# First expert's weights: w1 halves one per group in groups 1 to 8, w2 halves in pairs from group 15 to the tail

## The chip, the cores and the metric

The kernel runs on one core of a Trainium2 chip. The metric is the device time of one execution in microseconds, the median of the runs. Five engines work from queues of their own: TensorE (PE, with PEld for its weight loads), VectorE (DVE), ScalarE (ACT), GpSimd (POOL) and SyncE (SP, which here only issues DMAs). All DMAs share 16 DMA engines.

## The reference, cut to what matters

Attention in chunks of 64 rows gives 4608 rows of 512 numbers. Each row is then sent to the one of 8 experts whose gate logit is largest:

```
x = attn_out.transpose(0, 2, 1, 3).reshape(4608, 512)
logits = x @ w_gate
expert_idx = argmax(logits, axis=1)
for e in range(8):
    xe = x[expert_idx == e]
    h = maximum(xe @ w1[e], 0)        # w1[e]: 512 x 1024
    out[expert_idx == e] = gate_w * (h @ w2[e])   # w2[e]: 1024 x 512
```

## The kernel before, in words

**Attention, groups 0 to 17.** The 36 tiles of 128 rows are worked in 18 groups of two tiles (the loop over `g` at L1003). Group g computes the scores of its own tiles, transposes the probabilities of group g-1 (`attn_t`), multiplies them by V (`attn_v`), writes the result into a ring of row buffers `xb` (`x_out`), and transposes and projects the rows of group g-2 on the gate (`x_t`, `logits`). After the loop comes a tail, written out by hand from L1042, in which the last groups' steps alternate with pieces of the first expert's two matrix products (`filler`, 32 half steps in all, from `slot_0`).

**Routing and stores.** When a batch of 6 or 4 tiles has its logits, `route` computes each row's place in the sorted order, in small VectorE steps that `small_op` deals out. From then on `store` (L434) writes the rows to DRAM, one GpSimd indirect DMA for each tile (L441), at most two for each call; `store(2, after)` first has ScalarE copy one element of `after` into the row (L439), so that GpSimd doesn't send the row before that point. The row numbers of a batch lie in `di` (L418), a tile with two buffers, so a batch's `di` is written over the one of two batches before. After the last store, `gather(1)` (L1113, L569) reads the rows of slot 1 back in sorted order; `make_xt(1)` transposes them on PE (L591) and slot 1 begins. Slots 1 and up are the rest of the span.

**Weights of the first expert.** w1[0] and w2[0] lie in DRAM as four blocks of 128 x 2048; each is loaded in four pieces of 128 x 512 (256 KB), by `load_q(j)` on SP, where j = 0 to 7 is w1 and j = 8 to 15 is w2. They land in two staging buffers `raw[0]` and `raw[1]`; piece j uses the place of piece j-8 again. `split_half` makes two float32r tiles of a piece: ScalarE casts it (L84, the high part) and GpSimd subtracts that from the piece (L85, the low part). `cast(g)` (L996) first splits the pieces listed for g and then loads those listed for g. In the loop it is called behind the softmax of the group (L1027). w1 is needed from the first filler on, w2 from the fourth step of `slot_0`.

**Order.** PE, DVE, ACT and POOL keep the order in which the program lists their instructions. SP's queue holds, for each group, `cast`'s loads, then `load_qk(g+3)` (gated by the scores of group g, which free the buffer), then `load_v(g+2)` (gated by `attn_v` of group g-1). `cast`'s loads wait only for the staging place.

Of the kernel before, what the change touches and what calls it, by code (L numbers as in the profile page):

```python
# [47 lines left out]
def attn_moe_kernel(ctx: ExitStack, tc: tile.TileContext, q, k, v, wg, w, out):  # L48
# [31 lines left out]
    def split_half(c, m, buf, eng=None):  # L80

        hi, lo = w_hi[0][c][:, m * 512:(m + 1) * 512], w_lo[0][c][:, m * 512:(m + 1) * 512]
        src = raw[buf][:, (c % 2) * 1024 + m * 512:(c % 2) * 1024 + (m + 1) * 512]
        nc.scalar.copy(hi, src)  # L84
        (eng or nc.gpsimd).tensor_tensor(lo, src, hi.bitcast(F32), ALU.subtract)  # L85
# [13 lines left out]
    def bank(tag, shape):  # L99
        n = 1  # L100
        for x in shape[1:]:
            n *= x
        if tag == "S":
            t = psum[0].tile([P, 512], F32, name="psS", tag="S", bufs=2)
        else:
            t = slots[tag][turns[tag] % len(slots[tag])]
            turns[tag] += 1
        t = t[0:shape[0], 0:n]
        if len(shape) == 3:
            t = t.rearrange("p (a b) -> p a b", b=shape[2])  # L110
        return t
# [194 lines left out]
    def x_out(g, px, ri, xt):  # L306
        r0 = g * G % RB

        t = g * G - XB * RB
        assert t < 0 or t in stored  # L310
        for m in range(2):
            nc.vector.tensor_tensor(
                xt[:, r0:r0 + G, m * 256:(m + 1) * 256].rearrange("p i (h d) -> p i h d", d=64),
                px[m].rearrange("p (i h d) -> p i h d", i=G, d=64),
                ri.rearrange("p (i h m) o -> p i h m o", i=G, m=2)[:, :, :, m, :]
                .broadcast_to([P, G, 4, 64]), ALU.mult)

    def x_t(g, xt):
        xT = sp.tile([P, 4, G * P], F32, name="xT1", bufs=1)
        for i in range(G):  # L320
            pxt = bank("TQ", [P, 4, 128])
            for kc in range(4):
                nc.tensor.transpose(pxt[:, kc, :], xt[:, (g * G + i) % RB, kc * 128:(kc + 1) * 128],
                                    ident)
            nc.scalar.copy(xT[:, :, i * P:(i + 1) * P], pxt)
        return xT
# [4 lines left out]
    def logits_p(g, xT):  # L331

        pp = pL[:, 128:128 + G * P]
        for kc in range(4):
            nc.tensor.matmul(pp[kc * 32:(kc + 1) * 32, :], wg_sb[:, kc, :], xT[:, kc, :],
                             start=True, stop=True, tile_position=(0, kc * 32))
        lp = sp.tile([P, G * P], F32, name="lp", bufs=2)
        return lp, pp
# [95 lines left out]
    def store(n, after=None):  # L434

        for k, (b, i, t, di) in enumerate(waiting[:n]):
            x = xb[t // RB % XB][:, t % RB, :]
            if k == 0 and after is not None:
                nc.scalar.copy(x[:, XW - 1:XW], after)  # L439
            stored.add(t)  # L440
            nc.gpsimd.indirect_dma_start(  # L441
                out=xds[b % 2 * NMAX + i],
                out_offset=bass.IndirectOffsetOnAxis(ap=di[:, i, :], axis=0),
                in_=x, in_offset=None, bounds_check=NT - 1, oob_is_err=False)
        del waiting[:n]
# [4 lines left out]
    def advance(kind, side=False):  # L450


        for x in active:
            if x[1] == kind and x[2] == side and not (kind == "t" and r_live[0]):
                x[1] = next(x[0], "end")
                if x[1] == "end":
                    active.remove(x)
                return
# [3 lines left out]
    def small_op(n=1):  # L462

        for _ in range(min(n, pace[0])):
            advance("v")
            pace[0] -= 1
# [233 lines left out]
    def filler(n):  # L700
        for _ in range(n):
            next(fill, None)
            halves[0] -= 1
# [271 lines left out]
    def logits(g):  # L975
        if g in st_x:
            lp, pp = logits_p(g, st_x.pop(g))
            nc.scalar.copy(lp, pp)
            st_l[g] = lp

    def pauses():
        for x in list(active):
            if x[1] is None:
                x[1] = next(x[0], "end")
                if x[1] == "end":
                    active.remove(x)

    def load_q(j):

        c, s = j // 4, slice(j % 4 * 512, (j % 4 + 1) * 512)  # L990
        nc.sync.dma_start(raw[c % 2][:, s], w[c * E * P:c * E * P + P, s])

    loads = {g: [2 * g - 2, 2 * g - 1] for g in range(1, 9)}
    splits = {g: [2 * g - 6, 2 * g - 5] for g in range(3, 11)}

    def cast(g):  # L996

        for j in splits.get(g, ()):
            split_half(j // 2, j % 2, j // 4 % 2)
        for j in loads.get(g, ()):  # L1000
            load_q(j)
# [46 lines left out]
    g = NG - 1  # L1048
# [10 lines left out]
    soft_e(su)  # L1059
    advance("a")  # L1060
    st_x[g - 1] = x_t(g - 1, xb[(g - 1) * G // RB % XB])
    pauses()
    small_op(7)
    advance("a")
# [4 lines left out]
    ri = soft_d(su)  # L1069
    x_out(g, px, ri, xb[g * G // RB % XB])  # L1070
    logits(g - 1)
    store(2, st_l[g - 1][:, 0:1])
    filler(1)
    advance("t")
# [215 lines left out]
```

## Time and profile before

| what | us |
|---|---|
| median of 3 runs | 584.07 |
| the three runs | 581.40, 584.07, 587.08 |
| the profiled execution, its own time | 583.63 |
| its span | 581.5 |
| PE busy | 561.4 (97%) |
| DVE busy | 443.5 (76%) |
| ACT busy | 300.1 (52%) |
| POOL busy | 275.7 (47%) |

The span is the time from the program's first to its last instruction; 2.1 us of the execution's own time lie around it. Busy times are those of the profiled execution. PE's busy time is made from modelled ends of matmuls, so what counts is where it waits.

### The profile page before, as it was taken

To read this page: it belongs to the slowest core of one execution; us is meant where nothing else is said; L and a number is where in the kernel's file an instruction comes from. 1 tells how busy PE (TensorE), PEld (TensorE's weight loads), DVE (VectorE), ACT (ScalarE), POOL (GpSimd) and SP (SyncE) were. 2 spreads that over 40 slices of the span, in tenths; PEclk is the share of its full clock that TensorE was granted. 3 is DMA by queue.
4 is the path that set the end of the run, shared out by engine and by line. 5 is a ranking of instruction groups with operands and counts; after the bars stand their busy time and mean duration, and the time that the engine had idled before them with its cause. 6 is when DMAs were issued, how large, how long until landed. Compare 5 with 4: busy or idle time off the path is not lost.

```text
span 581.5 us, 13591 instructions
## 1 busy us (share of the span) xinstructions
PE 561.4 (97%) x5047; PEld 498.3 (86%) x5047; DVE 443.5 (76%) x834; ACT 300.1 (52%) x563; POOL 275.7 (47%) x279
## 2 busy tenths in 40 slices
PE   6999998999899999999999999999999999999995
PEld 6788877888788998989889899999988999899894
DVE  8899998976676877786776677877666787778775
ACT  1678755652144554563554455464434555456553
POOL 5056742447543754435355366444614444644352
PEclk9999999999999999999999999999999999999998
DMA  8999999425674732456246423368712245632121
GB/s 280 401 402 387 399 319 308 155 104 197 212 284 138 242 105 64 147 154 210 61 154 204 133 85 86 128 204 298 223 55 93 74 137 153 214 99 75 22 57 38
DMA packets 52510, 103.22 MB, mean 178 GB/s; under 512 B 15712, under 2 KB 32096, under 8 KB 48800
## 3 DMA queue, kind: packets, MB, share of 16 engines
q0 software_dynamic: 20704, 60.74, 30.8%
q1 hardware_dynamic: 31680, 40.93, 21.0%
q8 instruction: 63, 1.03, 0.7%
q14 instruction: 63, 0.52, 0.3%
HBM read 121.60 MB, written 19.82 MB: 243 GB/s over the span
## 4 chain that ended last, share of the span: by engine, by line
PE 67%; DMA 17%; issue 7%; POOL 4%; POOLq 3%; DVE 1%; ACT 0%; SPq 0%; DVEq 0%; ACTq 0%
PE psS L635 12%; DMA out_y<-y,oid 10%; PE psS L642 6%; PE psS L245 6%; DMA raw<-in_w,widx 6%; PE psV L713 4%; PE psU L713 4%; PE psU L714 3%; PE psL L635 3%; PE psV L714 3%; PE psU L715 3%; PE psV L715 3%; PE psU L300 3%; POOLq L1228 3%; POOL raw L551 2%
## 5 line engine op out<-in xcount | busy, mean ns | idle before, releaser
L78 DVE TENSOR_TENSOR wlo<-raw,whi 128x1024 fp32r<-128x1024 f32 x134 | 163.4, 1219 | 27.5 <-ACT whi L77 24.5
L77 ACT CAST whi<-raw 128x1024 fp32r<-128x1024 f32 x134 | 140.0, 1045 | 0.1
L551 POOL DMA_INDIRECT raw<-in_w,widx x70 | 89.0, 1271 | 103.1 <-DVE wlo L78 49.7
L635 PE MATMUL psS<-xhl,whi 128*128 128x256 f32 x688 | 127.3, 283 | 0.5 <-DVE xhl L594 0.3
L656 ACT ACTIVATE hh<-psS 128x256 fp32r<-128x256 f32 x110 | 42.3, 385 | 163.7 <-PE psS L635 115.7
L635 PEld LDWEIGHTS psS<-xhl,whi 128*128 128x128 f32 x688 | 111.7, 191 | 7.1 <-DVE xhl L594 0.5
L741 POOL DMA_INDIRECT out_y<-y,oid x40 | 49.5, 1237 | 103.4 <-ACT y L738 24.6
L635 PE MATMUL psS<-xhl,wlo 128*128 128x256 f32 x344 | 97.3, 283 | 0.0
L661 DVE SCALAR_TENSOR_TENSOR hl<-psS,hh 128x256 fp32r<-128x256 f32 x110 | 46.4, 422 | 49.0 <-ACT hh L656 31.0
L569 POOL DMA_INDIRECT xg<-xd,idx x58 | 69.6, 1199 | 22.6 <-issue 14.4
L635 PEld LDWEIGHTS psS<-xhl,wlo 128*128 128x128 f32 x344 | 65.6, 191 | 0.0
L713 PE MATMUL psU<-whi,hh 128*128 128x512 f32 x144 | 57.2, 397 | 1.2 <-ACT xhl L618 1.2
L713 PE MATMUL psV<-whi,hh 128*128 128x512 f32 x144 | 57.5, 399 | 0.3
L714 PE MATMUL psU<-wlo,hh 128*128 128x512 f32 x144 | 56.9, 395 | 0.0
L714 PE MATMUL psV<-wlo,hh 128*128 128x512 f32 x144 | 56.4, 392 | 0.0
L715 PE MATMUL psV<-whi,hl 128*128 128x512 f32 x144 | 56.2, 390 | 0.0
L715 PE MATMUL psU<-whi,hl 128*128 128x512 f32 x144 | 56.2, 390 | 0.0
L441 POOL DMA_INDIRECT xd<-xb,di x32 | 31.5, 985 | 22.8 <-issue 13.3
L635 PE MATMUL psL<-xhl,whi 128*128 128x256 f32 x208 | 38.5, 283 | 0.0
L642 PE MATMUL psS<-xhl,whi 128*128 128x320 f32 (+1 forms) x192 | 36.7, 316 | 0.5 <-ACT xhl L626 0.5
L85 POOL TENSOR_TENSOR wlo<-raw,whi 128x512 fp32r<-128x512 f32 x16 | 20.1, 1276 | 35.1 <-DMA spare<-in_k 20.4
L635 PEld LDWEIGHTS psL<-xhl,whi 128*128 128x128 f32 x208 | 33.2, 191 | 1.1
(244 smaller groups left out, 1082.6 us busy)
## 6 DMA issues: line engine op xcount, KB each, us to landing
qt<-in_q SPq DMA_DIRECT2D x17, 512.0 KB
xg<-xg SPq DMA_DIRECT2D x256, 32.0 KB
vb<-in_v SPq DMA_DIRECT2D x12, 512.0 KB
kb<-in_k SPq DMA_DIRECT2D x22, 256.0 KB
raw<-in_w SPq DMA_DIRECT2D x16, 256.0 KB
spare<-in_k SPq DMA_DIRECT2D x12, 256.0 KB
spare<-in_v SPq DMA_DIRECT2D x6, 512.0 KB
raw<-in_w,widx POOLq DMA_INDIRECT x70, 3.0
```

Of the source, the lines that this page charges most:

```text
L77: nc.scalar.copy(hi, src)
L78: nc.vector.tensor_tensor(lo, src, hi.bitcast(F32), ALU.subtract)
L551: nc.gpsimd.indirect_dma_start(out=raw[c][:, :], out_offset=None, in_=w, in_offset=bass.IndirectOffsetOnAxis(ap=widx[:, u, c:c + 1], axis= ...
L569: nc.gpsimd.indirect_dma_start(out=t[:, :], out_offset=None, in_=xd[0:rows, :], in_offset=bass.IndirectOffsetOnAxis(ap=place(u, h), axis=0 ...
L635: nc.tensor.matmul(ph, a, b[:, kc, 0:BLK], start=kc + i == 0, stop=kc + i == 5)
L642: nc.tensor.matmul(ph, a[par][kc][:, f * 128:(f + 1) * 128], b[:, kc, 0:BLK + n], start=kc + i == 0, stop=kc + i == 5)
L656: nc.scalar.activation(hh, ph, AF.Relu)
L661: nc.vector.scalar_tensor_tensor(hl, ph, 0.0, hh.bitcast(F32), ALU.max, ALU.subtract)
L713: nc.tensor.matmul(py, hh, wh, start=f == 0, stop=False)
L714: nc.tensor.matmul(py, hh, wl, start=False, stop=False)
L715: nc.tensor.matmul(py, hl, wh, start=False, stop=f == 7)
L741: nc.gpsimd.indirect_dma_start(out=outs[m], out_offset=bass.IndirectOffsetOnAxis(ap=oid[u % 3][0:n, m:m + 1], axis=0), in_=y, in_offset=No ...
```

## The change

Loads: in groups 1 to 8 one piece in place of two, so that these groups load w1 alone. The eight pieces of w2 are listed in pairs for g = 15, 16, 17 and 18. Splits: in groups 3 to 10 one piece in place of two; the pairs of w2 for g = 16, 17, 18 and 19. As the loop ends with g = 17, the tail gets two new calls of `cast`: `cast(18)` (there g is 17, so `cast(g + 1)`) behind the transpose `x_t` of group 16, and `cast(19)` behind the logits of group 16, ahead of the `store` that stands there. `cast(18)` splits two pieces and loads the last two; `cast(19)` splits the last two.

```diff
-    loads = {g: [2 * g - 2, 2 * g - 1] for g in range(1, 9)}
-    splits = {g: [2 * g - 6, 2 * g - 5] for g in range(3, 11)}
+    loads = {**{g: [g - 1] for g in range(1, 9)}, **{g: [2 * g - 22, 2 * g - 21] for g in range(15, 19)}}
+    splits = {**{g: [g - 3] for g in range(3, 11)}, **{g: [2 * g - 24, 2 * g - 23] for g in range(16, 20)}}
...
     st_x[g - 1] = x_t(g - 1, xb[(g - 1) * G // RB % XB])
+    cast(g + 1)
     pauses()
     small_op(7)
     advance("a")
...
     logits(g - 1)
+    cast(g + 2)
     store(2, st_l[g - 1][:, 0:1])
```

## Rows read from the trace of the kernel before

**Rows 1.** Busy time by stage: attention, tail, slots (us, engines busy, clock, DMA share, GB/s).

```profile
5.60:112.40 106.80, 100.21 (x2048) 84.44 (x2050) 96.31 (x176) 67.81 (x152) 45.42 (x59) 1.00 0.95 349
112.40:152.50 40.10, 37.62 (x413) 32.44 (x411) 28.09 (x108) 15.30 (x50) 23.29 (x31) 1.00 0.37 139
152.50:581.50 429.00, 420.12 (x2554) 378.19 (x2554) 314.74 (x551) 215.66 (x361) 201.96 (x163) 0.99 0.44 139
```

**Rows 2.** The same view, one row per group: groups 6, 7 and 10 to 14.

```profile
40.63:46.97 6.34, 6.34 (x135) 5.50 (x137) 6.20 (x11) 4.33 (x11) 2.51 (x2) 1.00 1.04 398
46.97:52.99 6.02, 6.02 (x127) 5.02 (x128) 5.75 (x10) 5.03 (x13) 4.47 (x7) 1.00 0.98 375
...
65.38:71.97 6.59, 6.29 (x127) 5.17 (x128) 5.68 (x10) 5.34 (x14) 4.86 (x7) 1.00 1.02 399
71.97:78.27 6.30, 6.13 (x126) 5.04 (x128) 5.97 (x12) 4.83 (x11) 4.69 (x5) 1.00 0.95 339
78.27:85.28 7.01, 6.40 (x136) 5.46 (x137) 6.37 (x14) 4.01 (x10) 2.40 (x5) 1.00 0.92 299
85.28:92.37 7.09, 6.09 (x127) 5.10 (x128) 5.36 (x11) 3.82 (x10) 1.95 (x2) 1.00 0.94 295
92.37:100.04 7.67, 6.18 (x126) 5.12 (x128) 6.63 (x16) 3.83 (x10) 2.14 (x3) 1.00 0.97 339
```

**Rows 3.** The chain that ended last, in group 14 (start, us, what).

```profile
94.63 1.49 issue
```

**Rows 4.** Timeline of SP: last w issue and the last two V.

```profile
52.95 1.35 SPq L991 DMA_DIRECT2D raw<-in_w  x2
...
99.56 0.33 SPq L221 DMA_DIRECT2D spare<-in_v  x1
105.90 0.33 SPq L221 DMA_DIRECT2D vb<-in_v  x1
```

**Rows 5.** Timeline of POOL in the tail (start, us, what, idle before and its end).

```profile
122.82 0.31 POOL L420 COPY xb<-ft 128x4 f32<-128x4 f32 x2 [3.80 <-DVE dst L413]
125.92 0.98 POOL L441 DMA_INDIRECT xd<-xb,di  x1 [2.79 <-ACT xb L439]
127.20 0.98 POOL L441 DMA_INDIRECT xd<-xb,di  x1 [0.31 <-DVE hl L661]
128.97 0.97 POOL L441 DMA_INDIRECT xd<-xb,di  x1 [0.79 <-issue]
...
132.04 0.98 POOL L441 DMA_INDIRECT xd<-xb,di  x1 [0.51 <-POOL xb L420]
...
143.84 0.98 POOL L441 DMA_INDIRECT xd<-xb,di  x1 [0.31 <-issue]
147.56 1.04 POOL L569 DMA_INDIRECT xg<-xd,idx  x1 [2.74 <-PE psS L635]
```

**Rows 6.** PE's timeline at the end of the tail.

```profile
149.84 0.39 PE L715 MATMUL psV<-whi,hl 128*128 128x512 f32 x1
151.05 0.75 PE L591 MATMUL psQ<-ident,xg 128*128 128x128 f32 x4 [0.82 <-DMA xg<-xd,idx]
```

**Rows 7.** The two instructions of a split, all 16 (ns min/median/max, first and last start).

```profile
L84 ACT CAST whi<-raw x16: 602/617/631, 28.6 to 72.4; 128x512 fp32r<-128x512 f32 x16
L85 POOL TENSOR_TENSOR wlo<-raw,whi x16: 1265/1276/1286, 29.3 to 73.8; 128x512 fp32r<-128x512 f32 x16
```

**Rows 8.** ACT's timeline in group 17 and where the tail would split.

```profile
118.76 0.37 ACT L978 COPY lp<-psL 128x256 f32<-128x256 f32 x1 [1.20 <-PE psL L335]
...
124.85 0.61 ACT L325 COPY xT<-psQ 128x512 f32<-128x512 f32 x1
```

**Rows 9.** DVE's timeline in the tail: `di` twice, and the longest SBUF operation.

```profile
130.18 0.19 DVE L418 TENSOR_REDUCE di<-dst 128x4 int32<-128x32 f32 x1 [0.82 <-DMA xd<-xb,di]
...
137.29 0.19 DVE L418 TENSOR_REDUCE di<-dst 128x4 int32<-128x32 f32 x1
...
142.91 0.61 DVE L854 TENSOR_TENSOR kb<-kb,thr 128x432 f32<-128x432 f32 x1
```

## Prediction

> **What bounds the kernel now.** I first cut the span into stages [rows 1]: attention to 112.4 us, the tail to 152.5, the slots to 581.5. PE is busy 98% of the slots, so whatever moves the start of slot 1 moves the end by the same amount, and the change touches nothing behind that start. Two stretches ahead of it matter.
>
> In the attention the next view is the same table by group [rows 2]. A group takes 6.02 us where nothing holds PE up (group 7), and 6.34 where a batch's routing matmuls join it (group 6). Groups 10 to 14 take 6.59, 6.30, 7.01, 7.09 and 7.67 us; group 12 has the routing. Against 6.02 and 6.34 that is 0.57 + 0.28 + 0.67 + 1.07 + 1.65 = 4.24 us lost. The chain of waits shows what it is: pauses called "issue", in the midst of the four transposes of one bank, where no semaphore can hold PE [rows 3]. They come while the DMA engines are over nine tenths busy. What the reader is to see is their place. The last w load is issued at 52.95 [rows 4]; groups 12 to 14 lose the most and run beside no w load at all, while groups 6 and 7, with two w loads each at 375 to 398 GB/s, lose nothing.
>
> In the tail, POOL's timeline [rows 5] runs up to the start of slot 1: the last store at 143.84, its end at 144.82, 2.74 us until its rows have landed, the gather at 147.56, and PE's transposes of the gathered rows at 151.05. PE runs out of filler at 150.23 and waits 0.82 us for that gather [rows 6]. So POOL, not PE, sets the start of slot 1, and PE has under 1 us to give.
>
> **The change part by part.** I count against the profiled execution: span 581.5, own time 583.63, 0.44 below the median of 584.07.
>
> *Groups 1 to 8 lose eight loads; groups 3 to 10 lose eight splits.* A split is 0.617 us of ACT and 1.276 of POOL [rows 7]. Neither engine ends a wait of PE in these groups: groups 6 and 7 keep the pure PE pace with two splits or loads each. Worth 0. The eight loads are 2.1 MB, 5.2 us of DMA at some 400 GB/s. The gain is bounded by the pauses: -4.24 us at most, if every one is an echo of a DMA backlog that the w loads built up. The loss: with less to load the backlog is gone some groups earlier, and the groups without backlog and with stores are the ones that pause, 0.28 to 1.65 us each (mean 0.85); three more such groups cost +2.6. I take 0: the groups nearest to what is left (12 to 14: Q, K, V and stores, no w) are there before and after.
>
> *The loads of w2.* SP passes them ahead of time, as they wait for nothing but a staging place that was freed by group 10. The pair of group 15 goes out behind the V load of 99.56, and the other six pieces behind that of 105.90 [rows 4], 0.67 us each: about 106.5 to 110.5, 1.6 MB or 4 us of DMA. All Q and K loads are issued by then, and the DMA share falls to 0.37 in the tail [rows 1]. All pieces are there before their casts. Cost 0; upper end one more pause of group 14's size, 1.65 us, in group 16.
>
> *Splits in groups 16 and 17.* ACT casts two pieces, 1.2 us, in each. In group 17 they stand ahead of the copy at 118.76, before which ACT idles 1.20 us [rows 8]: hidden, within 0.1 us. POOL subtracts 2 x 2 x 1.276 = 5.1 us. Ahead of the L420 copy at 122.82 and the store at 125.92 it has idle times of 3.80 and 2.79 us, 6.6 us [rows 5], and the work in between can slide: hidden. Without that cover it would go straight into the chain below.
>
> *`cast(18)`.* Its casts follow the copy of `xT` that ends at 125.46 [rows 8], so POOL's first subtraction can start at 125.46 + 0.62 = 126.1, and the pair ends at 126.1 + 2.55 = 128.6. Behind it in POOL's queue stands the store that now starts at 125.92. It starts at 128.75: +2.8 us. That it waits shows on nobody at first; what is queued behind it does.
>
> *`cast(19)`.* Two stores of 1.28 us pitch end at 131.0; the next pair of subtractions goes to 133.55; the store that stood at 128.97 starts at 133.7, +4.7 us: 0.5 of its 0.79 us idle time is used up. At 132.04 some 0.35 more of idle time is used up, so it moves to 136.45: +4.4. From there to the last store POOL has only the pauses of 0.15 to 0.31 that every store has, and the delay stays: last store 148.25, landed at 152.0, gather there, PE's transposes at 155.45 in place of 151.05.
>
> *Who else waits.* `di` of a batch waits for the stores of two batches before: at 130.18 DVE already waits 0.82 us for one [rows 9]. It moves to about 133.0, and the `di` of the last batch from 137.29 to about 140.8. DVE's queue stands still for some 3 us each time, and with it the last routing tables and the `hl` that PE's filler needs; PE may lose 2 us in the filler, which then ends near 152.2. That is still ahead of 155.45, so it costs nothing as long as the store chain is last. ACT's 2 x 1.2 us in the tail go the same way.
>
> The tail's bounds: 2.5 us (one pair hidden) and 5.1 us (all four subtractions exposed). I take the walk: +4.4.
>
> Sum: 0 + 0 + 4.4 gives 583.63 + 4.4 = 588.0 for an execution like the profiled one, and 584.07 + 4.4 = 588.5 for the median: 0.75% slower. Under 1% (5.8 us, about what a measurement of this kernel can tell from no change, as its three runs lie 5.7 us apart).
>
> **The rivals.**
>
> *A, not slower: the pauses were the w loads' doing.* The fewer bytes in groups 1 to 8 leave less outstanding in the DMA queues through group 14, and all 4.24 us come back: 588.5 - 4.2 = 584.3. For it: the pauses start right after the w loads, with the DMA share at 1.02 in group 10, and the profile lists a DMA queue for instructions. Against it: they grow while the DMA share falls, to 1.65 us six groups after the last w load. It decides if groups 12 to 14 come under 6.4 us. The Trainium skill (Runtime: NRT & Kernel Launch, Instruction fetch mechanics) says that an engine's instructions arrive by DMA in blocks of 256 and that crossing a block is mostly hidden; the trace agrees with the first (PE starts 254 to 255 instructions in a plain group, and pauses about once a group), not with "mostly hidden". By the page's "hidden" no load could move the pauses, and the sum stays as it is.
>
> *B, slower: the pauses spread.* Three more groups pause at the mean of 0.85, or the w2 burst adds one of 1.65 in group 16: 588.5 + 2.6 = 591.1. For it: no backlog is the state in which the pauses are long. Against it: the early groups have no stores beside their loads.
>
> *C, the tail hides it.* PE's order with the casts in it, or a later x transposition, moves other waits so that the stores are not last; the cost falls to PE's own wait, 0 to 1: 584.5. Against it: 0.82 us of slack at 151.05.
>
> *D, the subtractions get longer in the tail.* Each waits for a DVE operation of up to 0.61 us, the longest on SBUF there [rows 9]: 4 x 0.61 = 2.4, 590.9. Against it: the 16 subtractions of before stay within 1265 to 1286 ns [rows 7] while DVE is busy over nine tenths of the time (5.75 of 6.02 us in group 7) [rows 2]. The Trainium skill (SBUF — State Buffer, the shared port pair) has a rule of this kind: a VectorE operation with two SBUF inputs and a GpSimd operation that reads SBUF lock each other out. No row here shows it.
>
> *That the change doesn't do what it says* can be in one place: SP sends the loads of groups 16, 17 and the tail all at 106 us, not group by group. Its price is in B.
>
> **How the numbers follow.** Forecast 0.50; A 0.17; B 0.16; C 0.12; D 0.05. The forecast's own range is 586 to 590.5 (the tail's 2.5 to 5.1 and a median that moves by a microsecond). For 8 in 10 the range takes in C and most of A below and B above: 582.5 to 592. Slower by over 1% is above 589.9: a fifth of the forecast (0.10), two thirds of B and D (0.14): 0.24. Faster by over 1% is below 578.2, which needs A and C together and more: 0.03. The rest, 0.73, is within 1%.
>
> **What would show each step.** Right: the row of POOL's last L441 store starts about 4.4 us later than 143.84, counted from the start of group 17; four L85 rows stand between L420 and the L441 stores of the tail; PE waits about 3 to 5 us for `xg` ahead of L591; DVE's L418 rows wait for `xd`. Groups 12 to 14 still take 7 us. Wrong: groups 10 to 14 at 6.02 and 6.34 (A); groups 5 to 9 above 6.4 (B); no wait ahead of L591 (C); L85 rows over 1.5 us (D).

## The result and the profile after

The changed kernel takes 588.06 us (median of 21 runs, 585.62 to 596.79) and the kernel before 584.17 in the same measurement (21 runs, 580.48 to 587.28): 1.0069 of its time, 95% interval 1.0046 to 1.0092. Ratios here and below come from the runs in the faster of two states that executions have, and can differ a little from the quotient of the medians. The forecast was 588.5. The time came out, but by luck: the attention gains where I had put 0, the tail loses more than I had put down, and the two errors nearly cancel.

The profiled execution has a span of 587.6 us (own time 589.43). First its windows (us, engines busy, clock, DMA share, GB/s): group 1, groups 10 to 14 that answer to [rows 2], and the tail of [rows 1], with a piece of it.

```profile
12.36:18.56 6.20, 5.96 (x110) 5.48 (x110) 3.81 (x4) 2.33 (x5) 0.00 (x0) 0.74 1.03 418
67.69:73.77 6.08, 6.08 (x128) 5.09 (x124) 5.75 (x11) 4.54 (x12) 3.63 (x6) 1.00 0.97 352
73.77:79.86 6.09, 6.09 (x129) 5.10 (x125) 5.63 (x12) 4.63 (x11) 3.45 (x4) 1.00 0.94 336
79.86:86.20 6.34, 6.34 (x137) 5.50 (x134) 6.00 (x14) 4.04 (x10) 2.40 (x5) 1.00 0.97 346
86.20:92.22 6.02, 6.02 (x128) 5.10 (x125) 5.70 (x11) 3.75 (x10) 1.96 (x2) 1.00 0.98 343
92.22:98.24 6.02, 6.02 (x128) 5.09 (x125) 5.75 (x14) 3.84 (x10) 2.22 (x3) 1.00 1.00 352
112.40:152.50 40.10, 36.01 (x356) 30.37 (x353) 31.64 (x92) 16.62 (x53) 29.14 (x35) 0.87 0.34 133
131.70:141.90 10.20, 9.61 (x43) 7.92 (x42) 4.25 (x13) 2.65 (x11) 8.49 (x12) 0.50 0.40 157
```

The five groups that lost 4.24 us [rows 2] now run at or within 0.07 us of the pure pace: 6.08, 6.09, 6.34, 6.02, 6.02. PE is busy all the time in them. That is what rival A asked for (groups 12 to 14 under 6.4). The tail has lost in turn: PE's busy time in it falls from 37.62 to 36.01 us of 40.10, though its clock is at half for 10.2 us of them and makes the same work longer, and POOL's rises from 23.29 to 29.14 [rows 1].

SP's timeline shows where the w2 loads went; it answers to [rows 4].

```profile
98.26 1.20 SPq L991 DMA_DIRECT2D raw<-in_w  x2
104.17 0.33 SPq L221 DMA_DIRECT2D vb<-in_v  x1
104.59 3.25 SPq L991 DMA_DIRECT2D raw<-in_w  x6
```

Six of the eight pieces are sent in one go behind the last V load, a little before the 106.5 to 110.5 that I worked out, as PE's groups are earlier too.

POOL's timeline around the end of the attention and through the tail answers to [rows 5] (the last bracket of a row is the idle time before it and what ended it):

```profile
101.22 0.98 POOL L441 DMA_INDIRECT xd<-xg,di  x1 [3.56 <-issue]
102.51 0.97 POOL L441 DMA_INDIRECT xd<-xg,di  x1 [0.30 <-issue]
107.99 1.04 POOL L569 DMA_INDIRECT xg<-xd,idx  x1 [4.51 <-PE psL L969]
...
115.63 1.06 POOL L441 DMA_INDIRECT xd<-xg,di  x1 [4.86 <-DVE mx L260]
...
118.12 2.53 POOL L85 TENSOR_TENSOR wlo<-raw,whi 128x512 fp32r<-128x512 f32 x2
120.81 1.01 POOL L441 DMA_INDIRECT xd<-xb,di  x1 [0.17 <-POOL wlo L85]
...
123.12 2.53 POOL L85 TENSOR_TENSOR wlo<-raw,whi 128x512 fp32r<-128x512 f32 x2
125.71 0.30 POOL L420 COPY xb<-ft 128x4 f32<-128x4 f32 x2
125.97 2.50 POOL L85 TENSOR_TENSOR wlo<-raw,whi 128x512 fp32r<-128x512 f32 x2
128.63 1.00 POOL L441 DMA_INDIRECT xd<-xb,di  x1 [0.16 <-ACT whi L84]
129.94 0.98 POOL L441 DMA_INDIRECT xd<-xb,di  x1 [0.30 <-DVE ri L283]
130.93 2.52 POOL L85 TENSOR_TENSOR wlo<-raw,whi 128x512 fp32r<-128x512 f32 x2
133.61 0.99 POOL L441 DMA_INDIRECT xd<-xb,di  x1 [0.17 <-POOL wlo L85]
...
149.04 0.97 POOL L441 DMA_INDIRECT xd<-xb,di  x1 [0.30 <-ACT hh L656]
153.12 1.04 POOL L569 DMA_INDIRECT xg<-xd,idx  x1 [3.11 <-DVE o_a L885]
```

Read it from the top. POOL stands still 4.51 us ahead of the first gather (107.99) and 4.86 ahead of the store behind it (115.63). By the program's order it is a transfer that ends both waits, and not the engine that the bracket names: the gather needs the rows of the stores ahead of it in DRAM, and that store may write only when the gather has read. The gather's last packets move between 114 and 115 us, before between 112 and 113. Then POOL runs without a gap worth naming from 115.63 to 135, with all four pairs of subtractions between the stores. The pairs of groups 16 and 17 (118.12 and 123.12) stand in the tail as well: POOL has them in order behind the stores that wait for the first gather, which start in the tail before, too (113.84), and the late gather moves them further. PE's transposes of slot 1 (L591) start at 156.63 in place of 151.05 [rows 6], and without a wait: its filler, at half the clock for a part, ends no earlier than the gathered rows come. From the last gather to L591 it is 3.51 us, as before (3.49), so the chain of stores and gather sets the start here too.

To compare executions I count from the start of group 17, whose scores (L245) start at 112.34 before and at 110.61 after. The rows are those of the timelines of PE and POOL in each run. "Groups 2 to 16" is from the start of group 2 to that of group 17; the other columns are the start of the first store behind the first gather, of the last store, and of L591 in slot 1.

| profiled execution | groups 2 to 16 | store behind gather | last store | slot 1 |
|---|---|---|---|---|
| before | 95.93 | 1.50 | 31.50 | 38.71 |
| after | 92.05 | 5.02 | 38.43 | 46.02 |
| after, second profile (`after_again`) | 92.06 | 5.23 | 37.75 | 45.31 |
| after, third profile (`after_b`) | 92.18 | 7.53 | 41.22 | 48.89 |
| `tail_only` | 93.40 | 1.45 | 36.37 | 43.50 |
| `tail_dve` | 93.40 | 1.54 | 34.62 | 41.70 |
| `dve_tail` | 92.06 | 5.72 | 37.15 | 44.43 |
| `no_burst_b` | 92.11 | 5.82 | 38.58 | 46.14 |
| `loop_splits` | 92.36 | 6.07 | 33.97 | 41.18 |
| `early_pairs_b` | 94.67 | 5.09 | 31.77 | 38.83 |

The difference of the two spans, 6.1 us, is then: start of group 2 at 18.56 and not 16.41, +2.15; groups 2 to 16, -3.88; group 17 to slot 1, +7.31; the rest, +0.5. The first term is chance: the granted clock is at 0.74 in the group from 12.36 (first row above), and the second profile of the same kernel has group 2 at 16.25. Without it the sum is +3.9, which is also the difference of the medians. The second profile gives -3.87 and +6.60, the third -3.75 and +10.18; the medians that belong to the three profiles lie 3.9, 2.9 and 6.0 us over those of before.

### The profile page after: what moved, and what is told of

Its sections match the earlier page's. It is cut to its first block, busy times and chain, and to the rows that moved or that the text cites. A ratio compares the mean times of both kernels' runs of the same rounds, so it can differ in the third digit from the quotient of the medians.

```text
span 587.6 us, 13589 instructions
## 1 busy us (share of the span) xinstructions
PE 567.8 (97%) x5047; PEld 504.0 (86%) x5047; DVE 451.8 (77%) x834; ACT 299.2 (51%) x563; POOL 274.7 (47%) x279
## 5 line engine op out<-in xcount | busy, mean ns | idle before, releaser
L551 POOL DMA_INDIRECT raw<-in_w,widx x70 | 85.6, 1223 | 102.5 <-DVE wlo L78 46.8
L635 PE MATMUL psS<-xhl,whi 128*128 128x256 f32 x688 | 128.7, 285 | 1.8 <-DVE oid L584 1.4
L635 PEld LDWEIGHTS psS<-xhl,whi 128*128 128x128 f32 x688 | 113.1, 193 | 8.6 <-ACT at L292 1.6
L741 POOL DMA_INDIRECT out_y<-y,oid x40 | 52.0, 1299 | 103.6 <-ACT y L738 26.4
L85 POOL TENSOR_TENSOR wlo<-raw,whi 128x512 fp32r<-128x512 f32 x16 | 20.3, 1282 | 44.7 <-DMA kb<-in_k 27.5
L713 PEld LDWEIGHTS psV<-whi,hh 128*128 128x128 f32 x144 | 27.2, 189 | 8.6 <-issue 2.3
```

The costliest lines, as they stand in the source:

```text
L551: nc.gpsimd.indirect_dma_start(out=raw[c][:, :], out_offset=None, in_=w, in_offset=bass.IndirectOffsetOnAxis(ap=widx[:, u, c:c + 1], axis= ...
L635: nc.tensor.matmul(ph, a, b[:, kc, 0:BLK], start=kc + i == 0, stop=kc + i == 5)
L713: nc.tensor.matmul(py, hh, wh, start=f == 0, stop=False)
L741: nc.gpsimd.indirect_dma_start(out=outs[m], out_offset=bass.IndirectOffsetOnAxis(ap=oid[u % 3][0:n, m:m + 1], axis=0), in_=y, in_offset=No ...
```

## The experiments

The runs were taken in three series, each with its own runs of the kernel before. `splits` and `loads` are the two tables of the diff; pieces 0 to 7 are w1, 8 to 15 w2. Unless a diff is against another kernel, it is against the changed one.

**The change again (`after_again`).** No edit.

> The changed kernel itself, for a second profile. Theory 1 (the w loads of groups 1 to 8 caused the pauses of groups 10 to 14; the subtractions of the tail in GpSimd's queue make the last store late): again no pauses, groups at 6.02 to 6.35 us, and again about 7 us more from the start of group 17 to the transposes of slot 1 than before (45.8 against 38.7). Rival (the profile of the changed kernel was a chance: a late start of group 1 to 2 with the clock at half, and a clock at half from 131.7 to 141.9 us): the start is 2 us earlier, the clock stays up, and the tail is 43 us. Time 588 by both, within 1.5.

587.2 us against 584.34: 1.0061 (1.0029 to 1.0092). Its profile (span 584.6) has the fast groups again, and no loss at the start. So the fast attention and the long tail of the changed kernel repeat. Half the clock in the tail repeats as well, in other places (the rival had it stay up).

**Only the four tail pieces (`tail_only`).** The loads of the kernel before, splits of pieces 0 to 11 as before, pieces 12 to 15 where the change has them.

```diff
-    splits = {g: [2 * g - 6, 2 * g - 5] for g in range(3, 11)}
+    splits = {**{g: [2 * g - 6, 2 * g - 5] for g in range(3, 9)}, 18: [12, 13], 19: [14, 15]}
```

> The kernel before, but the last four pieces of w2 are split in the two new places in the tail; all loads stay in groups 1 to 8. Theory 1: the pauses of groups 10 to 14 stay (4 us in all), the tail is longer by the walk of the prediction, 4.4 us: 588.6. Rival 2 (what makes the tail longer is the burst of w2 loads on the DMA queues, not the subtractions): 584.2, no change.

590.72 us, 1.0114 (1.0073 to 1.0154). This is the walk of `cast(18)` and `cast(19)` by itself. POOL's timeline, the wait of PE, and DVE's two `di` rows:

```profile
123.51 2.54 POOL L85 TENSOR_TENSOR wlo<-raw,whi 128x512 fp32r<-128x512 f32 x2 [2.93 <-ACT whi L84]
126.19 1.00 POOL L441 DMA_INDIRECT xd<-xb,di  x1
...
145.84 1.00 POOL L441 DMA_INDIRECT xd<-xb,di  x1 [0.30 <-issue]
152.97 1.13 PE L591 MATMUL psQ<-ident,xg 128*128 128x128 f32 x4 [3.58 <-DMA xg<-xd,idx]
131.56 0.19 DVE L418 TENSOR_REDUCE di<-dst 128x4 int32<-128x32 f32 x1 [4.49 <-DMA xd<-xb,di]
138.14 0.19 DVE L418 TENSOR_REDUCE di<-dst 128x4 int32<-128x32 f32 x1 [2.77 <-DMA xd<-xb,di]
```

The last store is 4.87 us later than before, counted from group 17 (36.37 against 31.50); the walk said 4.4. PE waits 3.58 us for the gathered rows (predicted 3 to 5), and both `di` wait for `xd`, as the walk had it. What the changed kernel loses beyond that, 1.4 to 4.9 us at the last store in its three profiles, comes from elsewhere. PE's "issue" pauses are there as before, but not in the same place: groups 10 and 11 take 6.57 and 6.95 us, groups 12 to 14 take 6.35, 6.02 and 6.02.

```profile
71.76:78.71 6.95, 6.13 (x128) 5.05 (x124) 6.18 (x12) 3.95 (x10) 2.17 (x3) 1.00 0.93 340
```

**No split behind group 17 (`loop_splits`).** w2 pairs loaded in groups 13 to 16 and split in 14 to 17.

```diff
-    loads = {**{g: [g - 1] for g in range(1, 9)}, **{g: [2 * g - 22, 2 * g - 21] for g in range(15, 19)}}
-    splits = {**{g: [g - 3] for g in range(3, 11)}, **{g: [2 * g - 24, 2 * g - 23] for g in range(16, 20)}}
+    loads = {**{g: [g - 1] for g in range(1, 9)}, **{g: [2 * g - 18, 2 * g - 17] for g in range(13, 17)}}
+    splits = {**{g: [g - 3] for g in range(3, 11)}, **{g: [2 * g - 20, 2 * g - 19] for g in range(14, 18)}}
...
-    cast(g + 1)
...
-    cast(g + 2)
```

> w1 as in the changed kernel; the pairs of w2 are loaded in groups 13 to 16 and split in groups 14 to 17, nothing in the tail. Theory 1: no pauses (-4.2) and a tail as before or up to 1 us longer: 580 to 581. Rival 3 (w loads beside Q, K, V and stores bring the pauses back in groups 13 to 15): 583 to 585. Rival 2 has nothing against 580 to 582.

582.76 us, 0.9993 (0.9962 to 1.0024). The groups keep their gain (92.36), the tail loses 2.5 us, and they cancel to within what is measured. The store behind the first gather is as late as in the changed kernel (6.07), without the w2 loads of the tail; but here the pair of subtractions of group 15 stands in POOL's order ahead of that gather, and the last pair of w2 is still sent at 102.69, 4.8 us before it.

**The tail's subtractions on VectorE (`dve_tail`).**

```diff
-            split_half(j // 2, j % 2, j // 4 % 2)
+            split_half(j // 2, j % 2, j // 4 % 2, nc.vector if g > 17 else None)
```

> The changed kernel, but VectorE subtracts the four pieces of the tail, not GpSimd. Theory 1: the stores move up by most of the 5.1 us of subtractions, VectorE's 4 x 0.65 us cost under 1: 584 to 585. Rival 2 (burst of loads): 588, no change against the changed kernel. Rival 4 (VectorE's queue sets the tail as soon as GpSimd's doesn't): 586 to 587.

587.34 us, 1.006 (1.0024 to 1.0095): no gain over the change. With two pairs off POOL its last store still comes at 37.15. The late first gather is still there (5.72), the pairs of groups 16 and 17 as well. The time lies between the forecasts of rival 4 (586 to 587) and rival 2 (588) and doesn't part them.

**The second series.** The kernel before took 595.52 us there, 2% more than in the other series. Why isn't known; its profile (`before_again`) shows where. One of its groups (group 8):

```profile
56.71:63.67 6.96, 6.57 (x128) 5.42 (x125) 5.91 (x12) 4.63 (x11) 4.03 (x6) 1.00 0.96 302
```

Groups 7 to 15 take 6.9 to 8.1 us in all four kernels of that series. So the pauses aren't a property of the loads alone, and neither forecast of `before_again` can be judged by it.

> The kernel before itself, for a second profile. Theory 1 (its pauses come from the w loads of groups 1 to 8): groups 10 to 14 again lose about 4 us. Rival 5 (the pauses of groups 12 to 14 are a chance of one execution, as the run with the splits of the tail alone, which has the same loads, lost 1.5 us in groups 10 and 11 and nothing later): 1 to 2 us lost in groups 10 and 11, none in 12 to 14. Start of group 17 to slot 1: 38.7 by both.

Three orders of the loads ran in it. `no_burst` loads w2 in groups 11 to 14 and splits as the change does:

```diff
+    loads = {**{g: [g - 1] for g in range(1, 9)}, **{g: [2 * g - 14, 2 * g - 13] for g in range(11, 15)}}
```

> The changed kernel with the pairs of w2 loaded in groups 11 to 14 (split as in the changed kernel, in groups 16, 17 and twice in the tail), so that no w load stands on the DMA queues beside the first gather. Theory 1 with the burst as a second term: the first store behind the first gather comes 3 us behind the gather's copies, not 5 to 6, and the start of group 17 to slot 1 goes from 45.5 to 43.5: 585.5. Rival (GpSimd's four pairs in a row fill the tail whatever the gather does): 45 us, 587.5. Rival 3 (w loads beside Q, K, V bring pauses back in groups 11 to 14): 1 to 3 us more.

`early_pairs` loads w2 in groups 9 to 12 and splits nothing behind group 14 (both `cast` calls of the tail are gone, as in `loop_splits`):

```diff
+    loads = {**{g: [g - 1] for g in range(1, 9)}, **{g: [2 * g - 10, 2 * g - 9] for g in range(9, 13)}}
+    splits = {**{g: [g - 3] for g in range(3, 11)}, **{g: [2 * g - 14, 2 * g - 13] for g in range(11, 15)}}
```

> w1 one piece in each of groups 1 to 8, the pairs of w2 loaded in groups 9 to 12 and split in groups 11 to 14; the tail as before. Theory 1: no pauses and a tail of 38.7: the attention gains 3.5 to 4 us and nothing is lost, 580.5. Rival 3 (pairs beside Q, K, V and stores fill the DMA queues and the pauses come back in groups 10 to 14): 583 to 585.

`one_a_group` takes one piece in each of groups 1 to 16, again with nothing split in the tail:

```diff
+    loads = {g: [g - 1] for g in range(1, 17)}
+    splits = {**{g: [g - 3] for g in range(3, 17)}, 17: [14, 15]}
```

> One piece loaded in each of groups 1 to 16 and split two groups later (the last two in group 17), nothing in the tail. Theory 1: no pauses; the three splits in groups 16 and 17 and the last loads cost the tail 1 to 1.5 us: 581.5. Rival 3: one piece a group is enough for pauses behind group 8: 583 to 584.

`no_burst` 599.72, 1.0066 (1.0046 to 1.0085); `early_pairs` 595.73, 1.0007 (0.9989 to 1.0026); `one_a_group` 595.76, 1.0001 (0.9981 to 1.002). None of the three orders was faster. In the slow groups there was no gain to keep, and what split in the tail lost again: slot 1 is 47.9 us behind group 17 in `no_burst`, 43.1 in `before_again` (where 38.7 was expected).

**The third series: the parts again, at the usual times.** `after_b` is the change without an edit, `no_burst_b` and `early_pairs_b` are the kernels of the second series, and `tail_dve` is `tail_only` with the edit of `dve_tail`. The kernel before: 583.58 us.

> The changed kernel once more, as the yardstick of this call. Both theories: 2 to 5 us over the kernel before. Theory (the tail is a chain of GpSimd, lengthened by the four last subtractions and by the late first gather): in the tail GpSimd idles some 5 us between the first gather and the store that waits for it, and from there to the last store it is almost without a gap; last store 37.5 to 38.5 us behind the start of group 17, slot 1's transposes 45 to 46. Rival (the late gather is chance): about 3 us of idle time there.

> The changed kernel with its w2 halves loaded in pairs in groups 11 to 14 instead of 15 to 18, all splits where the change has them. Theory (w2 loads late in the attention hold up the first gather's landing): the idle time of GpSimd behind the first gather falls from some 5 to about 3 us, the splits of groups 16 and 17 then lie in idle time, and only the four last pieces lengthen the chain (+4.4 us by the walk): 1.5 to 2.5 us faster than the changed kernel of this call, still 1 to 3 us over the kernel before. Rival (only the four last pieces count, the late gather costs nothing): as the changed kernel, within 0.7 us.

> The loads of the kernel before, pieces 12 to 15 split where the change splits them (groups 18 and 19), their subtractions on VectorE and not on GpSimd. The same with the subtractions on GpSimd took 1.0114 of the time before. Theory (GpSimd's turn in the tail is what the four subtractions cost): nothing is put between the stores, no gather is late, so the last store comes 31 to 33 us behind the start of group 17 and slot 1's transposes 38.5 to 40.5; the time is that of the kernel before, within 1.5 us. Rival (the casts on ScalarE, or the loads of w1 two a group, are what costs): 4 to 7 us over the kernel before, as with GpSimd.

> One w1 half a group as in the change, w2 halves in pairs in groups 9 to 12, split in pairs in groups 11 to 14, nothing of the split behind group 17's start. Theory (the change gains in groups 10 to 14 and loses in the tail): the gain without the loss, 1 to 4 us under the kernel before, no group from 3 on over 6.4 us but those with routing, slot 1's transposes 38.5 to 41 us behind the start of group 17. Rival (the pauses come and go from run to run, whatever is loaded): the time of the kernel before, within 1 us.

`after_b` 589.6, 1.0096 (1.0067 to 1.0125); `no_burst_b` 588.69, 1.0073 (1.0042 to 1.0105); `tail_dve` 586.99, 1.0063 (1.0038 to 1.0088); `early_pairs_b` 584.43, 1.0006 (0.9974 to 1.0038).

*A late gather needs no burst.* In the changed kernel the burst does stand in its way. Two rows of the DMA view of `after`, from the gather at 107.99 to 111.00 (packets, MB, share of the 16 DMA engines; q1 is the queue of SP's loads, q0 that of GpSimd's stores and gathers):

```profile
q1 hardware_dynamic: 554, 1.03, 93.6%
q0 software_dynamic: 2, 0.01, 3.3%
```

In `no_burst_b` no packet of q1 moves from the gather at 106.95 to the store behind it at 114.51:

```profile
q0 software_dynamic: 160, 0.54, 26.1%
```

Yet the store is as late. POOL's rows of `no_burst_b`, then of `after_b`:

```profile
100.60 0.97 POOL L441 DMA_INDIRECT xd<-xg,di  x1 [0.30 <-issue]
106.95 1.04 POOL L569 DMA_INDIRECT xg<-xd,idx  x1 [5.38 <-PE psT L323]
...
114.51 1.05 POOL L441 DMA_INDIRECT xd<-xg,di  x1 [4.77 <-ACT whi L84]
```

```profile
101.53 0.98 POOL L441 DMA_INDIRECT xd<-xg,di  x1 [0.30 <-issue]
...
117.15 1.05 POOL L441 DMA_INDIRECT xd<-xg,di  x1 [7.93 <-ACT lp L978]
```

I expected 3 us of idle time ahead of the store at 114.51; it is 4.77, and the gather itself waits 5.38 instead of 2.79 before. From the second store of group 15 to the store behind the gather it is 9.60 us before, 9.55 in `tail_only` and 9.63 in `tail_dve`, and 13.12 in the change, 13.97 in `loop_splits`, 13.91 in `no_burst_b`, 12.77 in `early_pairs_b`, 15.62 in `after_b`. The first three load two pieces a group and have sent the last by group 8; the others load one a group and send w2 later. That is what they differ in, burst or not; it isn't shown to be the cause. In the second series the gather of `early_pairs`, the same kernel as `early_pairs_b`, isn't late (9.51), and that of `one_a_group` hardly (10.11). So in the changed kernel the w2 loads are shown beside the gather; what makes it late without them stays open. The times of `no_burst_b` and `after_b` can't be told apart.

*The splits cost with VectorE's subtractions too.* `tail_dve` lies at 1.0063 where `tail_only` was at 1.0114 in another series (their intervals overlap); its last store is 3.12 us late instead of 4.87. ACT's rows, DVE's, and POOL's store that is released by them:

```profile
122.35 1.17 ACT L84 CAST whi<-raw 128x512 fp32r<-128x512 f32 x2
124.69 0.23 ACT L388 ACTIVATE eg<-lg 128x32 f32<-128x32 f32 x1 [1.16 <-DVE lg L365]
124.82 0.14 ACT L439 COPY xb<-psU 128x1 f32<-128x1 f32 x1
123.03 1.29 DVE L85 TENSOR_TENSOR wlo<-raw,whi 128x512 fp32r<-128x512 f32 x2 [1.90 <-ACT whi L84]
124.25 0.18 DVE L363 TENSOR_REDUCE lm<-lg 128x4 f32<-128x32 f32 x1
125.24 0.98 POOL L441 DMA_INDIRECT xd<-xb,di  x1 [5.08 <-ACT hh L656]
```

DVE stands 1.90 us at the subtraction until ACT has cast, and only then goes on to `lm` and `lg`; ACT's `eg` waits for `lg`, and behind `eg` stands the copy L439 that POOL's store needs. Taken off one engine's queue, the work stands in the queues of two others ahead of the same store. I had expected the time of before.

*The pauses don't come back; VectorE is late in their place.* `early_pairs_b` has a tail as short as before (38.83), but groups 13 to 16, behind its w2 loads, lose 2.6 us against the 6.02, 6.02, 6.34 and 6.02 of the changed kernel. Groups 13 and 15:

```profile
83.74:90.97 7.23, 6.09 (x129) 5.10 (x125) 6.96 (x14) 4.42 (x13) 4.88 (x7) 1.00 1.03 409
97.47:104.25 6.78, 6.41 (x134) 5.50 (x134) 6.48 (x14) 4.81 (x12) 4.83 (x6) 1.00 0.60 216
```

These aren't the pauses called "issue": PE waits for `ex` of the softmax ahead of the scores of each of groups 14 to 17 (1.14, 0.35, 0.36 and 0.41 us). VectorE is busy 6.96 us of group 13, and one of its small operations stands for as long as a GpSimd subtraction runs beside it. PE's row, VectorE's and GpSimd's:

```profile
90.97 1.97 PE L245 MATMUL psS<-spare,qt 128*64 128x128 f32 x32 [1.14 <-DVE ex L263]
86.19 1.20 DVE L510 TENSOR_TENSOR ge<-pid_h,c 128x6 f32<-128x6 f32 x1
84.86 2.51 POOL L85 TENSOR_TENSOR wlo<-raw,whi 128x512 fp32r<-128x512 f32 x2 [1.83 <-ACT whi L84]
```

The same operation takes 0.17 us in the changed kernel, which splits nothing there. So in group 13 at least, what costs is a split beside VectorE's work, and not a load. I had forecast the time 1 to 4 us under that of before.

PE's waits over the attention can now be counted in all ten profiles outside the second series. From 28 us to the start of group 17 "issue" pauses stand in the three that load two pieces a group in groups 1 to 8 (before, `tail_only`, `tail_dve`), and in none of the seven that load one, whatever they load behind group 8. (In the profile of before one of the pauses, 1.0 us in group 13, is put down to ScalarE's copy L439 and not called "issue".)

`early_pairs_b` is no faster than before, and no version here is shown to be.

## Why the prediction came out, and where it was wrong

*Groups 1 to 8 lose eight loads, "worth 0": wrong.* The bounds were -4.24 to +2.6; it is -3.88 against the profile of before, and the same in all three profiles of the change (92.05 to 92.18). Against `tail_only` and `tail_dve`, which load as before, it is only -1.3 (93.40). Their profiled executions lie 3.2 and 2.3 us under the medians of their kernels, that of before 0.5 under its own, so the size of the gain in the median stays open. Rival A had the mechanism, with its measure (groups under 6.4), at 0.17: the pauses go when groups 1 to 8 load one piece each. My argument against it was the false step: that groups 12 to 14 lose the most and "run beside no w load at all" came from one profile. In `tail_only` and `tail_dve` the loss lies in groups 10 to 12 (1.5 and 1.8 us), and 13 and 14 lose nothing. As the splits of groups 3 to 10 went from two to one with the loads, no run parts the two. And pairs of loads don't make pauses by themselves: `early_pairs_b` has them in groups 9 to 12, `no_burst_b` in 11 to 14, without one. The Trainium skill (Runtime: NRT & Kernel Launch, Instruction fetch mechanics) calls the crossing of an instruction block mostly hidden; the pauses, up to 1.65 us in a group, aren't hidden if they are such crossings, which no run isolates. In the second series none of the orders took them away.

*The w2 loads, "cost 0": wrong, in a place that I hadn't looked at.* PE isn't held up; the first gather is, and in the changed kernel the loads have nine tenths of the DMA engines just then (93.6% against 3.3%). POOL's first gather and the store behind it take 3.5 us more in the change (13.12 against 9.60), and 3.2 to 6.0 more in each version of the first and third series with w loads behind group 8, for which the cause is open. In the second series `no_burst` has 10.50 against 9.75 of `before_again`. The late gather costs nothing by itself: in `early_pairs_b` the store is 3.6 us late and the last store 0.3, as POOL's idle time takes it up. I had looked for who waits for the pieces and not for who else uses the DMA engines then: the DMA share that I relied on was that of the tail, and the gather lies ahead of it.

*Splits in groups 16 and 17, "hidden": wrong for POOL.* The cover was 6.6 us of idle time [rows 5]. The late gather takes 3.5 of it, and then the 5.1 us of subtractions have to go into what is left: 3.5 + 5.1 - 6.6 gives 2.0 us too much, and with the 4.87 of `tail_only` 6.9 at the last store, as measured. The same estimate gives 7.1 for `after_again`, 9.4 for `after_b`, 7.7 for `no_burst_b` and, without the 4.87, 3.1 for `loop_splits`, where 6.3, 9.7, 7.1 and 2.5 were measured. No run has these splits with a gather in time, so that they would be hidden then is not shown. From the store behind the gather to the last store POOL needs 33.4 us (115.63 to 149.04) where it needed 30.0, together +6.9. I had said that without the cover the work goes straight into the chain below; it did, for these 2 us.

*`cast(18)` and `cast(19)`, +4.4: right, a little small.* `tail_only` gives 4.87 at the last store. The place of each pair between the stores, the waits of both `di` and PE's wait are as predicted there. In the whole change PE's wait is gone, as PE is late itself.

*The bounds of the tail, 2.5 to 5.1:* the change lies at +6.6 to +10.2 from group 17 to slot 1, outside. In sum: -3.9 + 6.6 = +2.7 by the second profile, where I had 0 + 4.4. That the median came within half a microsecond of the forecast is luck: two terms that I had put at 0 have opposite signs.

*Rival B* didn't come: no group from 3 on takes over 6.4 us. *C:* only PE's wait is hidden, not the delay. *D:* the rule shows, but the other engine pays: the L85 rows stay near 1.27 us each (2.50 to 2.53 a pair), and VectorE's operations get longer; it is the section below. *That SP sends the loads all at 106 us* is true for six of eight (104.59).

## What to carry to other kernels

Before you call a moved load free, list every queue that has a transfer of its own in the window that it moves into, and what stands in order behind that transfer; here it was a gather, and more than half of the idle time that was to hide other work went into waiting for it. Idle time ahead of a work that is bound to come late isn't cover: take off what the change itself delays, and only then see what fits. Work that is taken off the engine at the end of a chain may stand in the order of an engine that feeds the same chain. And when a stretch gets slower again, look at what PE waits for before you call it the same loss.

## What the hardware showed that I had not expected

*A small VectorE operation is held while GpSimd subtracts.* DVE's timeline of the changed kernel, beside POOL's pairs at 118.12, 123.12 and 125.97, and then the view of line L369 (ns min/median/max, first and last start):

```profile
118.33 2.35 DVE L407 TENSOR_SCALAR gs<-gs 128x4 f32<-128x4 f32 x1
123.77 1.94 DVE L365 TENSOR_TENSOR lg<-lg,lm 128x32 f32<-128x32 f32 x1
125.74 2.78 DVE L369 SCALAR_TENSOR_TENSOR eq<-lg,iota_m 128x32 f32<-128x32 f32 x1
```

```profile
L369 DVE SCALAR_TENSOR_TENSOR eq<-lg,iota_m x7: 191/208/2781, 41.5 to 139.2; 128x48 f32<-128x48 f32 x4, 128x32 f32<-128x32 f32 x3
```

An operation of some 0.2 us takes 1.94 to 2.78 and ends within 0.1 us of the pair (118.33 + 2.35 = 120.68; 118.12 + 2.53 = 120.65). POOL's pair keeps its 2.5 us. In `after_b` two pairs follow each other closely, and one operation is held for both:

```profile
124.53 5.50 DVE L365 TENSOR_TENSOR lg<-lg,lm 128x32 f32<-128x32 f32 x1
```

Whether two subtractions in a row are parted differs. In the attention of before, beside a pair that runs from 41.29 to 43.80, an operation that takes 0.2 us elsewhere ends with the first of the two, at 42.63:

```profile
41.65 0.98 DVE L380 TENSOR_TENSOR lo<-am,iota_m 128x48 bf16<-128x48 f32 x1
```

The Trainium skill (SBUF — State Buffer, SBUF: two separate sides) says that the first to start gets the port pair for its whole instruction and the other blocks. The trace agrees where VectorE's row starts behind the pair (118.33 and 123.77). The rows at 125.74 and 124.53 start 0.2 and 0.1 us ahead of it and wait all the same; the view doesn't show when an operation asked for the port. In the tail the cost isn't isolated: `tail_only` has no such row there and its stores are 4.87 us late all the same. In `early_pairs_b` it shows in PE's wait of 1.14 us for `ex`.

*TensorE's clock falls to half in the tail, and PE's waits alone don't explain it.* It is at half (0.50 in the windows, the 1.2 GHz level) from 131.70 to 141.90. In the 6.90 us ahead of that PE is busy 5.62, with a wait of 1.0 us for `oh_b` (129.02); a wait of 1.4 for `oid` (121.42) lies further ahead. PE of before is busy all of a like stretch (126.53 to 133.43) and keeps 1.00 through the tail. But in `loop_splits` PE is busy only 1.97 of the 4.00 us from 116.95, and 1.00 stays through its tail. The price isn't isolated: PE then comes to the gathered rows without a wait, so a faster filler alone would have ended in one.
